# Attention and a gated feed-forward layer on one core: other places for block 2's outputs, GpSimd splits in two runs, a burst one step later, whole weight stores

## The chip, the core and the metric

The kernel runs on one core of a Trainium2 chip. The metric is the device time of one execution in microseconds (us). Before the change three runs took 887.02, 887.28 and 889.04, median 887.28. The engines are TensorE (PE; its weight loads are listed as PEld), VectorE (DVE), ScalarE (ACT), GpSimd (POOL) and SyncE (SP), which issues nearly all transfers. Each engine works through its own instructions in order; semaphores tie the engines together.

## The reference

Attention within chunks of 64 positions (8 batches, 8 heads, 576 positions, head size 64), then a gated feed-forward layer on the 4608 tokens, all in float32.

```python
scores = scale * np.matmul(q_c, k_c.transpose(0, 1, 2, 4, 3))
scores = scores - np.max(scores, axis=-1, keepdims=True)
attn = np.exp(scores)
attn = attn / (np.sum(attn, axis=-1, keepdims=True) + 1e-09)
out = np.matmul(attn, v_c)                                    # -> x, 4608 x 512
...
g = x @ w_gate                                                # 512 -> 1536
silu = g * (1.0 / (1.0 + np.exp(-g)))
val = x @ w_val
return (silu * val @ w_out).astype(np.float32)                # 1536 -> 512
```

## The kernel before

**Blocks and pairs.** The tokens are taken in nine blocks of 512. Blocks 0 and 1 are done in an opening, block 2 alone, and blocks 3 to 8 in three pairs (`b` = 3, 5, 7). While one pair is in its gated layer, the attention of the next pair (`n` in the code, its two halves `c = n.a[0]` and `n.a[1]`) is done beside it; the last pair has none beside it.

**Splits.** Float32 products are made of three TensorE products of rounded parts: a number is split into an upper part (a rounding copy on ScalarE) and a lower one (a subtraction on VectorE or GpSimd). `split`, `Left.lower`, `lower`, `x_lower`, `halves` and `split_sums` are such places.

**Gated steps.** `gated_steps` (L1302) takes a pair through twelve steps `f` = 0 to 11, one for each 128 columns of the hidden layer. A step makes seven products instead of eight (Strassen's scheme on the pair's two blocks), here called product 0 to 6 in TensorE's order: `seventh(ps1, ..., 0)`, `(ps2, ..., 1)`, `(ps1, ..., 2)`, `(ps3, ..., 3)`, `(ps1, ..., 4)`, `(ps2, ..., 5)`, `(ps1, ..., 6)`, each six matmuls of 128x512 (L859). Product 2 goes on in the bank of product 0, and so waits until ScalarE has copied that (`rows`, L1315); likewise product 4 waits for the copy of `v1` (L1319), product 5 for that of `v2` (L1317), and product 6 until VectorE has added product 4 to `v2` (L1328, `add`, L863). VectorE's three adds (L863), two multiplications (`times`, L518) and one split (`hl`, L1193) are each step's own work; ScalarE has three copies, two `Silu`, and the split's copy (`hh`, L1190). `v1` and `v2` lie in one tile whose place is `ts` in even steps and `wo1` in odd ones (L1312).

**The projection lags.** Each step's hidden rows are multiplied by the output weights in the step after (`turns`, `project`, L531; `Left.project`, L1207), in four tiles of 128 tokens. For a pair they add up in the banks `ps_o`. In step 0 of the first pair the projection is that of block 2's last step: it finishes block 2, ScalarE copies each of the four results to `o_sb` (L550) and SP stores it (L551). The copies' buffers came by turns from two pools, `hp` (tag `o_sb`, two buffers, which the weights `left` of odd steps also use) and `ld` (tag `v_t`).

**Bursts.** Next to a step's own work stands the attention of the next pair, by the dictionaries `bursts`, `middle`, `mid` and `behind` of the loop at L1539. A burst is 128 small TensorE products: scores in two of the steps (L291), weighted values in two others (L369). In a step with a burst, the projection's tile 0 stands ahead of product 6, tile 1 behind it, then the burst, then tiles 2 and 3; in another step all four tiles stand ahead of product 6. After a burst of scores ScalarE copies one half of them out of the banks (`take`, L299) and VectorE subtracts the maxima of both (`less_top`, L306, L307). One step later ScalarE does the exponents (`middle`, L312) and VectorE the sums and the division (`normalize`), and in the steps after that VectorE turns the result, eight turns of four transposes each (L356): `mid` is ahead of `hl`, `behind` at the step's end. To some steps belongs a combination of hidden rows on VectorE (`s3`, `s1_of`, L1346), needed after the twelve steps.

**GpSimd.** In block 2 GpSimd prepares combinations of the gate weights (`LateQuarters`). There and beside the first pair's steps 0 to 7 it also prepares six combinations of the output weights: `out_sums` makes the sums, `split_sums` (L1161) splits them, with ScalarE's copy first and GpSimd's subtraction over 128x1024 after it (L1165), and stores them. In the pair's steps the sums stand in even steps and the splits in odd ones.

**Stores of weights.** `save_w` (L198) puts the split gate weights of each `f` into DRAM, from where `load_factors` and `again` fetch them: 1 MB for the first four `f`, and for the other eight only the three quarters that are read later, in two transfers of 512 and 256 KB.

**x of the first pair.** The pair's seven combinations of x are split in block 2's last steps (`pair.x0` to `pair.x6`, `halves`, L1077). Product `i` of a step reads `x[i]`.

**The order.** On PE, ACT and DVE the program's order is the engine's order. The instructions of SP and POOL are placed by a scheduler, which moves a transfer forward when its buffer comes free early.

Of the kernel before, what the change touches and what calls it, by code (L numbers as in the profile page):

```python
# [8 lines left out]
F32 = mybir.dt.float32  # L9
# [5 lines left out]
ALU = mybir.AluOpType  # L15
AX = mybir.AxisListType

P = 128
# [3 lines left out]
DM = H * D  # L22
# [11 lines left out]
def attn_then_gated_ffn(ctx: ExitStack, tc: tile.TileContext, qk, v, wgv, wo, out):  # L34
# [163 lines left out]
    def save_w(f):  # L198
        kept_w[f] = store.tile([P, 2, 4 * Q], F32, name=f"w{f}")
        for at in (slice(0, 4 * Q),) if f < EARLY else (slice(0, 2 * Q), slice(3 * Q, 4 * Q)):  # L200
            nc.sync.dma_start(out=kept_w[f][:, :, at], in_=w_both[f][:, :, at].bitcast(F32))
# [329 lines left out]
    def project(parts, wo_f, which=range(T)):  # L531
# [6 lines left out]
        for t in which:  # L538
            ts, o = slice(t * P, (t + 1) * P), a.o[t]
            nc.tensor.matmul(o, hl[:, ts], woh, start=f == a.steps[0], stop=False)  # L540
            nc.tensor.matmul(o, hh[:, ts], wol, start=False, stop=False)  # L541
            nc.tensor.matmul(o, hh[:, ts], woh, start=False, stop=f == a.steps[1])  # L542
            if f == a.steps[1]:

                pools = (hp, "o_sb"), (ld, "v_t")
                r = a.b * N + t * P

                pool, tag = pools[t % 2]
                o_sb = pool.tile([P, DM], F32, name="o_sb", tag=tag)
                nc.scalar.activation(o_sb, o, AF.Copy, scale=2.0 ** -8)  # L550
                nc.sync.dma_start(out=out[r:r + P, :], in_=o_sb)  # L551
# [609 lines left out]
    def split_sums(j, engine=nc.gpsimd):  # L1161
# [3 lines left out]
        engine.tensor_tensor(out=lo, in0=sums, in1=t, op=ALU.subtract)  # L1165
# [136 lines left out]
    def gated_steps(pair, middle, mid, behind, bursts, nothing=lambda: None):  # L1302
        for f in range(NF):
# [42 lines left out]
            for at, what, j in ((3, pair.s3, 0), (4, pair.s1_of, 0), (8, pair.s3, 1), (9, pair.s1_of, 1), (10, pair.s3, 2)):  # L1346
                if f == at:
                    what(j)
# [143 lines left out]
    def load_late(a):  # L1492
        with tc.issue_after(a.asked):
# [11 lines left out]
              11: lambda: (load_weights(1), load_queries_of(5), pair.x5(), pair.x6())}  # L1505
# [33 lines left out]
    for b in range(3, NB, 2):  # L1539
        n, middle, mid, behind, bursts = None, {}, {}, {}, {}  # L1540
        if b + 2 < NB:
# [6 lines left out]
            bursts = {0: lambda: scores(c, tiles=(q0, q2), first=2), 5: lambda: scores(n.second(), first=2),  # L1548
                      8: lambda: cross(c, first=2), 10: lambda: cross(n.a[1], first=2)}
            middle = {1: lambda: c.exponents(0, NP), 6: lambda: n.a[1].exponents(0, NP)}  # L1550
            mid = {2: turned(c, 0, 1), 3: turned(c, 3, 1), 4: turned(c, 6, 1),
                   7: lambda: turn_some(n.a[1], 0, 1), 8: lambda: turn_some(n.a[1], 3, 1), 9: lambda: turn_some(n.a[1], 6, 1)}
            behind = {1: lambda: c.normalize(0, NP), 2: turned(c, 1, 2), 3: turned(c, 4, 2), 4: turned(c, 7, 1),
                      6: lambda: (n.a[1].normalize(0, NP), load_values(c)), 7: lambda: turn_some(n.a[1], 1, 2),
                      8: lambda: (turn_some(n.a[1], 4, 2), load_values(n.a[1])), 9: lambda: turn_some(n.a[1], 7, 1)}
        if b == 3:
            for i in range(8):
# [37 lines left out]
```

## Time and profile before

| | us |
|---|---|
| runs (three): lowest, median, highest | 887.02, 887.28, 889.04 |
| the profiled execution | 885.88 |
| its span, first to last instruction | 884.1 |
| TensorE busy in the span | 868.6 |
| VectorE, ScalarE, GpSimd busy | 642.0, 418.4, 94.8 |
| first pair's steps 0 to 11 | about 328 to 476 |
| second pair's steps 0 to 11 | about 520 to 661 |

Rows of the timeline read: start in us, duration in us, engine, source line, operation, output<-input, shapes, how often, and in brackets the idle time of the engine ahead of it with what ended it. A row can stand for several like instructions in a run; its start is that of the first one, its duration that of all. In the list of waits the columns are: who waited, for whom, the sum in us, how often, the longest. `SPq` rows are the issues of transfers, not the transfers. In names from the profile the banks of a burst are called `ps_a` wherever they lie.

### The profile page before, as it was taken

What the parts mean: (1) busy time and instruction counts of PE and PEld (TensorE: products, weight loads), DVE (VectorE), ACT (ScalarE), POOL (GpSimd) and SP (SyncE); (2) the same over time, 40 slices, a digit from 0 to 9 for tenths busy, and PEclk for the clock granted to TensorE, in tenths of its full rate; (3) what the DMA queues carried; (4) which work ended last, traced back from release to release, by engine and by line L of the source; (5) the groups of instructions that cost most, each with busy time, mean ns of one, the idle gap of its engine ahead of it and who ended that gap; (6) DMA issues with size and microseconds to landing.
All of it is one profiled execution on the core that took longest, in us unless ns stands there. A gap on an engine that the chain in (4) does not pass through costs nothing.

```text
span 884.1 us, 16286 instructions
## 1 busy us (share of the span) xinstructions
PE 868.6 (98%) x6679; PEld 749.9 (85%) x6679; DVE 642.0 (73%) x898; ACT 418.4 (47%) x609; POOL 94.8 (11%) x72
## 2 busy tenths in 40 slices
PE   7999999999999998999999999999999999999998
PEld 6788888888878787888789998888889988888898
DVE  6888999673888764897977957878769744434674
ACT  5757777543533444435335635334346433333351
POOL 1100000000057722344100000000000000000000
PEclk9999999999999999999999999999999999999999
DMA  9768778888997896788766897565657675555552
GB/s 359 274 249 294 267 282 296 308 285 340 316 356 224 282 327 190 238 268 285 235 202 216 276 298 208 191 212 193 182 207 236 195 225 192 182 200 189 189 187 93
DMA packets 111530, 215.50 MB, mean 244 GB/s; under 512 B 32224, under 2 KB 71648, under 8 KB 102496
## 3 DMA queue, kind: packets, MB, share of 16 engines
q1 hardware_dynamic: 110016, 211.84, 70.5%
q10 hardware_dynamic: 1440, 2.62, 0.8%
q8 instruction: 52, 0.85, 0.4%
q14 instruction: 22, 0.18, 0.1%
HBM read 166.72 MB, written 47.71 MB: 243 GB/s over the span
## 4 chain that ended last, share of the span: by engine, by line
PE 87%; DVE 5%; DMA 4%; ACT 1%; issue 1%; SPq 0%; POOL 0%; DVEq 0%; ACTq 0%
PE ps_a L859 26%; PE ps_gv L859 19%; PE ps_o L1207 14%; PE ps_gv L479 9%; PE ps_gv L1207 6%; PE ps_o L540 3%; PE ps_o L541 3%; PE ps_o L542 3%; DMA qk_t<-in_qk 2%; DVE turned L356 2%; PE ps_a L291 1%; PE ps_a L369 1%; DMA out<-o_sb 1%; DMA t<-th 1%; DVE rows L518 1%
## 5 line engine op out<-in xcount | busy, mean ns | idle before, releaser
L859 PE MATMUL ps_a<-x,factors 128*128 128x512 f32 x864 | 217.2, 391 | 5.1 <-ACT rows L1315 3.0
L859 PEld LDWEIGHTS ps_a<-x,factors 128*128 128x128 f32 x864 | 159.3, 188 | 37.6 <-ACT rows L1315 3.9
L859 PE MATMUL ps_gv<-x,factors 128*128 128x512 f32 x648 | 164.4, 389 | 0.0
L859 PEld LDWEIGHTS ps_gv<-x,factors 128*128 128x128 f32 x648 | 121.6, 188 | 25.3
L479 PE MATMUL ps_gv<-xh,w 128*128 128x512 f32 x320 | 97.9, 391 | 0.2 <-ACT xh L614 0.2
L356 DVE STREAM_TRANSPOSE turned<-s_sb 32x256 f32<-32x256 f32 x192 | 83.6, 436 | 2.6
L1207 PE MATMUL ps_o<-sums,halves 128*128 128x256 f32 x630 | 76.6, 283 | 0.0
L1207 PEld LDWEIGHTS ps_o<-sums,halves 128*128 128x128 f32 x630 | 76.0, 192 | 0.0
L479 PEld LDWEIGHTS ps_gv<-xh,w 128*128 128x128 f32 x320 | 59.8, 188 | 12.9 <-ACT xh L614 0.5
L863 DVE TENSOR_TENSOR rows<-rows,ps_gv 128x512 f32<-128x512 f32 x36 | 24.7, 686 | 59.2 <-PE ps_gv L859 57.6
L518 DVE SCALAR_TENSOR_TENSOR rows<-v,rows 128x512 f32<-128x512 f32 x72 | 55.3, 769 | 12.2 <-ACT rows L1339 5.0
L479 PE MATMUL ps_gv<-xl,w 128*128 128x512 f32 x160 | 61.4, 393 | 0.0
L1190 ACT CAST hh<-rows 128x512 fp32r<-128x512 f32 x36 | 22.3, 620 | 82.3 <-DVE rows L518 82.3
L1250 DVE TENSOR_TENSOR halves<-rows,halves 128x1024 fp32r<-128x1024 f32 x36 | 43.5, 1221 | 18.5 <-ACT halves L1246 18.5
L540 PE MATMUL ps_o<-both,hl 128*128 128x512 f32 x144 | 56.5, 392 | 0.0
L542 PE MATMUL ps_o<-both,hh 128*128 128x512 f32 x144 | 56.1, 389 | 0.0
L541 PE MATMUL ps_o<-both,hh 128*128 128x512 f32 x144 | 56.0, 389 | 0.0
L1207 PE MATMUL ps_o<-left,hh 128*128 128x256 f32 x288 | 53.8, 283 | 0.0
L1207 PE MATMUL ps_gv<-sums,halves 128*128 128x256 f32 x432 | 53.3, 283 | 0.0
L1326 ACT ACTIVATE rows<-rows 128x512 f32<-128x512 f32 x36 | 22.8, 632 | 63.7 <-DVE rows L863 63.6
L1207 PEld LDWEIGHTS ps_gv<-sums,halves 128*128 128x128 f32 x432 | 52.7, 192 | 0.2
L1246 ACT CAST halves<-rows 128x1024 fp32r<-128x1024 f32 x36 | 37.3, 1049 | 28.3 <-PE ps_gv L1207 9.4
(166 smaller groups left out, 1407.4 us busy)
## 6 DMA issues: line engine op xcount, KB each, us to landing
factors<-t SPq DMA_DIRECT2D x36, 1024.0 KB, 7.2
factors<-w SPq DMA_DIRECT2D x36, 512.0 KB, 4.1
sums<-s SPq DMA_DIRECT2D x15, 1024.0 KB, 5.0
t<-th SPq DMA_DIRECT2D x24, 512.0 KB, 4.2
raw<-in_wgv SPq DMA_DIRECT2D x11, 1024.0 KB, 8.7
both<-o SPq DMA_DIRECT2D x22, 512.0 KB, 7.2
qk_t<-in_qk SPq DMA_DIRECT2D x20, 512.0 KB, 7.1
left<-o SPq DMA_DIRECT2D x36, 256.0 KB, 4.5
```

The costliest lines, as they stand in the source:

```text
L356: nc.vector.transpose(out=self.turned[to:to + 32, p:p + 2, j, :, 32 * (i % 2):32 * (i % 2) + 32], in_=src[32 * i:32 * i + 32, :, o // 2, 3 ...
L479: nc.tensor.matmul(ps, w, x, start=first and (k, i) == which[0], stop=last and (k, i) == which[-1])
L518: nc.vector.scalar_tensor_tensor(out=h, in0=pv, scalar=2.0 ** -8, in1=h, op0=ALU.mult, op1=ALU.mult)
L540: nc.tensor.matmul(o, hl[:, ts], woh, start=f == a.steps[0], stop=False)
L541: nc.tensor.matmul(o, hh[:, ts], wol, start=False, stop=False)
L542: nc.tensor.matmul(o, hh[:, ts], woh, start=False, stop=f == a.steps[1])
L859: nc.tensor.matmul(ps, w[u][:, k], x[i][v][:, k], start=first and k == 0 and n == 0, stop=k == NK // 2 - 1 and n == 2, skip_group_check=True)
L863: nc.vector.tensor_tensor(out=t, in0=t, in1=ps, op=ALU.add)
L1207: nc.tensor.matmul(to, a[:, ts], w[:, i], start=first and n == 0, stop=last and n == 2, skip_group_check=True)
L1246: nc.scalar.copy(out=t[:, 0], in_=src)
L1250: nc.vector.tensor_tensor(out=lo, in0=src, in1=hi.bitcast(F32), op=ALU.subtract)
L1326: nc.scalar.activation(h, h, AF.Silu, scale=2.0 ** -8)
```

## The change

Five edits.

1. Block 2's four outputs: tiles 0 and 1 go to the two halves of one tile at `wo1`, tiles 2 and 3 to the two buffers of `v_t`. `hp`'s `o_sb` is left to the weights `left`.
2. `split_sums`: the subtraction on GpSimd is made in two instructions of 128x512 in place of one of 128x1024. All six splits are concerned.
3. The burst of scores for the next pair's first block goes from step 0 to step 1, its exponents from step 1 to 2, its division from 1 to 2, and its eight turns from steps 2 to 4 to steps 3 to 6 (three, three, one, one). The second block's burst stays in step 5, its exponents and division in step 6, its turns in steps 7 to 9. `s1_of(0)` goes from step 4 to step 9. This holds for the first two pairs; the third has no next pair, but its `s1_of(0)` moves too.
4. `save_w` stores every `f` whole, 1 MB in one transfer.
5. The split of the first pair's x[6] goes from block 2's last step into step 0, behind the copy of `v1`.

```diff
     def save_w(f):
         kept_w[f] = store.tile([P, 2, 4 * Q], F32, name=f"w{f}")
-        for at in (slice(0, 4 * Q),) if f < EARLY else (slice(0, 2 * Q), slice(3 * Q, 4 * Q)):
-            nc.sync.dma_start(out=kept_w[f][:, :, at], in_=w_both[f][:, :, at].bitcast(F32))
+        nc.sync.dma_start(out=kept_w[f], in_=w_both[f].bitcast(F32))
...
-                pool, tag = pools[t % 2]
-                o_sb = pool.tile([P, DM], F32, name="o_sb", tag=tag)
+                if a.b != 2:
+                    pool, tag = pools[t % 2]
+                    o_sb = pool.tile([P, DM], F32, name="o_sb", tag=tag)
+                else:
+                    if not t:
+                        a.out = const.tile([P, 2, DM], F32, name="o_sb", tag="wo1")
+                    o_sb = a.out[:, t] if t < 2 else ld.tile([P, DM], F32, name="o_sb", tag="v_t")
                 nc.scalar.activation(o_sb, o, AF.Copy, scale=2.0 ** -8)
                 nc.sync.dma_start(out=out[r:r + P, :], in_=o_sb)
...
-        engine.tensor_tensor(out=lo, in0=sums, in1=t, op=ALU.subtract)
+        for at in (slice(0, 2), slice(2, 4)):
+            engine.tensor_tensor(out=lo[:, at], in0=sums[:, at], in1=t[:, at], op=ALU.subtract)
...
-            for at, what, j in ((3, pair.s3, 0), (4, pair.s1_of, 0), (8, pair.s3, 1), (9, pair.s1_of, 1), (10, pair.s3, 2)):
+            for at, what, j in ((3, pair.s3, 0), (9, pair.s1_of, 0), (8, pair.s3, 1), (9, pair.s1_of, 1), (10, pair.s3, 2)):
...
-              11: lambda: (load_weights(1), load_queries_of(5), pair.x5(), pair.x6())}
+              11: lambda: (load_weights(1), load_queries_of(5), pair.x5())}
...
-            bursts = {0: lambda: scores(c, tiles=(q0, q2), first=2), 5: lambda: scores(n.second(), first=2),
+            bursts = {1: lambda: scores(c, tiles=(q0, q2), first=2), 5: lambda: scores(n.second(), first=2),
                       8: lambda: cross(c, first=2), 10: lambda: cross(n.a[1], first=2)}
-            middle = {1: lambda: c.exponents(0, NP), 6: lambda: n.a[1].exponents(0, NP)}
-            mid = {2: turned(c, 0, 1), 3: turned(c, 3, 1), 4: turned(c, 6, 1),
+            middle = {2: lambda: c.exponents(0, NP), 6: lambda: n.a[1].exponents(0, NP)}
+            mid = {3: turned(c, 0, 1), 4: turned(c, 3, 1), 5: turned(c, 6, 1), 6: turned(c, 7, 1),
...
-            behind = {1: lambda: c.normalize(0, NP), 2: turned(c, 1, 2), 3: turned(c, 4, 2), 4: turned(c, 7, 1),
+            behind = {2: lambda: c.normalize(0, NP), 3: turned(c, 1, 2), 4: turned(c, 4, 2),
...
         if b == 3:
+            middle[0] = pair.x6
             for i in range(8):
                 behind[i] = sums_behind(i, behind.get(i, lambda: None))
```

The engines' orders at the places that the prediction speaks of. ScalarE in the first pair's step 0, before; `rows<-ps_a` in the list is `Silu` of product 6, `s_sb<-ps_a` the copy of the burst's scores, and the last row is step 1's first copy:

```order
L62 CAST x<-s_sb 128x1024 x2
L1315 COPY rows<-ps_a 128x512
L1317 COPY v<-ps_gv 128x512
L1319 COPY v<-ps_a 128x512
L1326 ACTIVATE rows<-rows 128x512
L1190 CAST hh<-rows 128x512
L550 ACTIVATE o_sb<-ps_o 128x512
L1339 ACTIVATE rows<-ps_a 128x512
L550 ACTIVATE o_sb<-ps_o 128x512
L299 COPY s_sb<-ps_a 128x8x64 x2
L550 ACTIVATE o_sb<-ps_o 128x512 x2
L1315 COPY rows<-ps_a 128x512
```

The same place now:

```order
L62 CAST x<-s_sb 128x1024
L1320 COPY rows<-ps_a 128x512
L1322 COPY v<-ps_gv 128x512
L1324 COPY v<-ps_a 128x512
L62 CAST x<-s_sb 128x1024
L1331 ACTIVATE rows<-rows 128x512
L1195 CAST hh<-rows 128x512
L554 ACTIVATE o_sb<-ps_o 128x512 x4
L1344 ACTIVATE rows<-ps_a 128x512
L1320 COPY rows<-ps_a 128x512
```

One split of x has moved behind the three copies, the four outputs stand together, and the copy of the scores has left the step. VectorE at the change from step 4 to step 5 (of both pairs), before; the adds to `rows` and `v` (L863) begin a step's work, L1224 is a combination of hidden rows, here `s1_of(0)`, and `top` is the burst's first maximum:

```order
L1193 TENSOR_TENSOR hl<-rows,hh 128x512
L518 SCALAR_TENSOR_TENSOR rows<-v,rows 128x512
L356 STREAM_TRANSPOSE turned<-s_sb 32x2x4x32 x4
L1224 TENSOR_TENSOR rows<-rows 128x1024
L863 TENSOR_TENSOR rows<-rows,ps_gv 128x512
L863 TENSOR_TENSOR v<-v,ps_a 128x512
L863 TENSOR_TENSOR v<-v,ps_gv 128x512
L518 SCALAR_TENSOR_TENSOR rows<-v,rows 128x512
L1193 TENSOR_TENSOR hl<-rows,hh 128x512
L518 SCALAR_TENSOR_TENSOR rows<-v,rows 128x512
L306 TENSOR_REDUCE top<-ps_a 128x8
```

And now:

```order
L1198 TENSOR_TENSOR hl<-rows,hh 128x512
L517 SCALAR_TENSOR_TENSOR rows<-v,rows 128x512
L355 STREAM_TRANSPOSE turned<-s_sb 32x2x4x32 x8
L867 TENSOR_TENSOR rows<-rows,ps_gv 128x512
L867 TENSOR_TENSOR v<-v,ps_a 128x512
L867 TENSOR_TENSOR v<-v,ps_gv 128x512
L517 SCALAR_TENSOR_TENSOR rows<-v,rows 128x512
L355 STREAM_TRANSPOSE turned<-s_sb 32x2x4x32 x4
L1198 TENSOR_TENSOR hl<-rows,hh 128x512
L517 SCALAR_TENSOR_TENSOR rows<-v,rows 128x512
L305 TENSOR_REDUCE top<-ps_a 128x8
```

Step 4 ends with two turns in place of one turn and the combination `s1_of(0)`, and step 5 has a turn between the multiplication and `hl`, ahead of the burst's maxima. Last, SP around block 2's outputs, before; `factors` are the weights of step 2, `v_t` values for the next pair's attention:

```order
L1130 DMA factors<-w_818 128x2x512
L1130 DMA factors<-w_818 128x2x256
L1130 DMA factors<-t_3147 128x2048
L551 DMA out<-o_sb 128x512 x2
L271 DMA v_t<-in_v 128x4x64
L551 DMA out<-o_sb 128x512 x2
```

And now:

```order
L1134 DMA factors<-w_818 128x2x512
L1134 DMA factors<-w_818 128x2x256
L555 DMA out<-o_sb 128x512 x3
L1134 DMA factors<-t_3139 128x2048
L555 DMA out<-o_sb 128x512
L270 DMA v_t<-in_v 128x4x64
```

Three of the four stores now go ahead of the last part of the weights (1 MB). Further ahead on SP, in block 2, one transfer of `left` (256 KB, step 3's) now stands before the loads of the first pair's second block, as its buffer no longer serves for an output.

## The prediction

> **What bounds the kernel now.** The page first: TensorE is busy for nearly the whole span, so the end moves only by what TensorE waits, or by work that comes to wait in front of it.
>
> ```profile
> span 884.1 us, 16286 instructions
> PE 868.6 (98%) x6679; PEld 749.9 (85%) x6679; DVE 642.0 (73%) x898; ACT 418.4 (47%) x609; POOL 94.8 (11%) x72
> ```
>
> The list of waits with TensorE as the one that waits (columns: sum in us, times, longest) then says what those waits are. These are its rows outside the opening:
>
> ```profile
> PE ps_a L859 <- ACT rows L1315: 3.0, 2, 2.7
> PE ps_a L291 <- DMA qk_t<-in_qk: 1.5, 3, 0.6
> PE ps_a L859 <- DVE v L863: 1.4, 1, 1.4
> ...
> PE ps_a L369 <- DVE h L518: 1.0, 1, 1.0
> ...
> PE ps_a L859 <- ACT s_sb L299: 0.7, 1, 0.7
> ...
> PE ps_a L291 <- ACT rows L1339: 0.2, 1, 0.2
> ```
>
> Of the 1.5 only one wait (0.6) lies outside the opening. So some 6.9 us in all can be won (3.0 + 0.6 + 1.4 + 1.0 + 0.7 + 0.2). The timeline shows where each comes from. First the first pair's steps 0 and 1:
>
> ```profile
> 329.88 1.05 ACT L62 CAST x<-s_sb 128x1024 fp32r<-128x1024 f32 x1 [1.76 <-DMA t<-th]
> ...
> 339.27 0.34 SPq L1130 DMA_DIRECT2D factors<-t  x1
> ...
> 339.97 1.31 SPq L551 DMA_DIRECT2D out<-o_sb  x2
> ...
> 347.34 1.08 ACT L550 ACTIVATE o_sb<-ps_o 128x512 f32<-128x512 f32 x2 [4.22 <-DMA out<-o_sb]
> ...
> 348.95 1.66 PE L859 MATMUL ps_a<-x,factors 128*128 128x512 f32 x6 [2.71 <-ACT rows L1315]
> ```
>
> Block 2's third output needs the buffer of its first, whose store is on the way, so ScalarE stands still for 4.22 with the copies of step 1 behind it, and TensorE loses 2.71. The other 0.3 of that row is step 0: the split of x[6] (the first line) waits for a store, and the copy `rows` stands behind it. Then steps 7 and 8 of that pair:
>
> ```profile
> 423.39 0.68 DVE L863 TENSOR_TENSOR v<-v,ps_a 128x512 f32<-128x512 f32 x1
> ...
> 424.13 3.01 PE L859 MATMUL ps_a<-x,factors 128*128 128x512 f32 x12
> ...
> 425.38 1.78 DVE L356 STREAM_TRANSPOSE turned<-s_sb 32x256 f32<-32x256 f32 x4
> ...
> 427.63 2.51 POOL L1165 TENSOR_TENSOR sums<-sums 128x1024 fp32r<-128x1024 f32 x1 [9.28 <-ACT sums L1164]
> 427.80 2.89 DVE L518 SCALAR_TENSOR_TENSOR rows<-v,rows 128x512 f32<-128x512 f32 x1
> ...
> 435.65 1.65 PE L859 MATMUL ps_a<-x,factors 128*128 128x512 f32 x6 [1.36 <-DVE v L863]
> ```
>
> Product 6 of a step rewrites the bank that VectorE's add of v2 reads. In step 7 that add ends at 424.07 and the product starts at 424.13: no room at all, and no loss. In step 8 VectorE comes 1.36 late, after standing 2.2 beside GpSimd's split (2.89 for an operation of 0.69). Last, the second pair's burst in step 0, which has no projection behind it to cover ScalarE's copy of the scores:
>
> ```profile
> 533.42 1.66 PE L859 MATMUL ps_a<-x,factors 128*128 128x512 f32 x6 [0.73 <-ACT s_sb L299]
> ```
>
> **What the change takes away.** The outputs' new places end the 4.22, if the stores land in time (rival A): -2.71. x[6] behind the step's third copy: -0.3; its 1.05 on ScalarE and an operation on VectorE then lie beside products 3 to 5, and it is first read by product 6. The burst in step 1 has two tiles of projection behind it, as the burst of step 5 has, and that one costs nothing; in the second pair this saves 0.73 and the 0.2 of the list's last row, 0.93. The rows of step 5's burst in the first pair, in which no wait stands before TensorE's two products, and the burst itself (in the second pair):
>
> ```profile
> 402.82 0.69 DVE L307 TENSOR_TENSOR s_sb<-ps_a,top 128x512 f32<-128x512 f32 x1
> ...
> 403.48 1.60 PE L859 MATMUL ps_a<-x,factors 128*128 128x512 f32 x6
> ...
> 404.92 1.53 PE L859 MATMUL ps_gv<-x,factors 128*128 128x512 f32 x6
> ```
> ```profile
> 587.82 2.10 PE L291 MATMUL ps_a<-qk_t 64*64 64x64 f32 x128
> ```
>
> For the split in runs of 512, what matters is whether VectorE gets in between two GpSimd instructions. It does so in step 6:
>
> ```profile
> 413.05 1.29 POOL L1156 TENSOR_TENSOR sums<-right 128x512 f32<-128x512 f32 x1
> ...
> 413.63 1.26 DVE L518 SCALAR_TENSOR_TENSOR rows<-v,rows 128x512 f32<-128x512 f32 x1 [0.95 <-ACT rows L1326]
> ...
> 414.42 1.62 POOL L1157 TENSOR_TENSOR sums<-sums 128x512 f32<-128x512 f32 x1
> ...
> 415.58 1.02 DVE L1193 TENSOR_TENSOR hl<-rows,hh 128x512 fp32r<-128x512 f32 x1 [0.69 <-ACT hh L1190]
> ```
>
> VectorE started at 413.63, waited for the GpSimd operation to end (414.34) and was done 0.55 later, while GpSimd's next one took 1.62 against 1.29. So a collision costs VectorE at most a run of about 1.3 instead of one of 2.5: some 1.2 less, which is nearly all of step 8's 1.36. [...]
>
> The same helps in block 2, where x's halves wait for a split:
>
> ```profile
> 296.47 3.39 POOL L1165 TENSOR_TENSOR sums<-sums 128x1024 fp32r<-128x1024 f32 x1
> ...
> 300.87 0.68 DVE L518 SCALAR_TENSOR_TENSOR h<-ps_gv,h 128x512 f32<-128x512 f32 x1
> ...
> 301.60 2.08 PE L369 MATMUL ps_a<-turned,v_t 64*64 64x64 f32 x124 [0.99 <-DVE h L518]
> ```
>
> But VectorE's operation reads the product that TensorE makes right before this multiplication, which it reached at 301.60 - 0.99 = 300.61, so the operation's 0.68 stays: I count 0.3 of the 0.99 (none to 0.99). Removed: 2.71 + 0.3 + 1.36 + 0.3 + 0.93 = 5.6.
>
> **What it adds.** Each thing that moved a step later now stands nearer to something else on VectorE. Two rows price it: the combination s3 that now stands with three turns right after the normalizing, and the projection's four tiles that TensorE does ahead of product 6 in a step without a burst (one tile of them, 0.36, in a step with one).
>
> ```profile
> 384.90 1.23 DVE L1224 TENSOR_TENSOR rows<-rows 128x1024 f32<-128x1024 f32 x1
> ```
> ```profile
> 448.85 1.43 PE ps_o L1207 x12
> ```
>
> First pair. Steps 1 to 4 now repeat what steps 5 to 8 were: burst, normalizing, three turns, three turns. Step 3 is like step 7: no loss. Step 4 is like step 8, with 1.23 more for s3, 1.2 less for the runs, and product 6 coming 1.07 later: 1.36 + 1.23 - 1.2 - 1.07 = 0.3. Its lateness is not made up before step 5, whose product 6 comes after one tile again: I put 0.6 (0 to 1.0). Step 5 has a new turn (1.78) ahead of the scores' maxima; 0.69 of it fills a wait for `hh`, so 1.1 shows. The bank that TensorE wants next was free at 402.82 + 0.69 = 403.51 and is taken at 404.92: 1.4 of room, no loss. Step 6's new turn again adds 1.1, of which it covers some 0.3 of the waits for GpSimd, and step 7 had no room: 0.8 (0.2 to 1.3). Step 8 keeps 1.36 - 1.2 = 0.2 (0 to 0.5). Sum 1.9, bounds 0.2 to 3.6.
>
> Second pair: no GpSimd, and room in step 7. The add of v2 ends at 609.81 and TensorE takes the bank at 611.31, 1.5 later, more than 1.1: nothing. `s1_of(0)` in step 9 is another 1.23, but that step has two turns where steps 3, 4 and 8 have three, 1.78 less: nothing.
>
> ```profile
> 609.13 0.68 DVE L863 TENSOR_TENSOR v<-v,ps_a 128x512 f32<-128x512 f32 x1
> ...
> 611.31 2.91 PE L859 MATMUL ps_a<-x,factors 128*128 128x512 f32 x12
> ```
>
> Whole weight stores: eight stores carry 256 KB more, eight issues fall away. TensorE waits for no transfer until the scores in block 2 (the 0.6). Ahead of that load go one store and, by the new order on SP, one `left` of 256 KB. Rows of the page, the issues and the timeline:
>
> ```profile
> GB/s 359 274 249 294 267 282 296 308 285 340 316 356 224 282 327 190 238 268 285 235 202 216 276 298 208 191 212 193 182 207 236 195 225 192 182 200 189 189 187 93
> ```
> ```profile
> w<-w SPq DMA_DIRECT2D x8, 256.0 KB, 6.1
> ```
> ```profile
> 243.48 1.22 SPq L201 DMA_DIRECT2D w<-w  x2
> ```
>
> At the 356 GB/s of that slice 256 KB are 0.74, twice 1.5; one issue less gives back about 0.6 to 0.8. I take +0.7 (-0.2 to 1.5). [...]
>
> **Sum.** -5.6 + 1.9 + 0.7 = -3.0. The profiled execution took 885.88 (span 884.1, 1.78 around it), so it would come to 882.9; it lies 1.4 under the median of the runs, 887.28, and the same 3.0 from the median gives **884.3**.
>
> **Rivals.**
> A. The wait is only moved. The outputs of tiles 0 and 1 now lie in the buffer that step 1's v1 and v2 use. If their stores land as late as they did, ScalarE stands in step 1 before v2. Landing of the first two outputs, and of the last two, as the transfers' rows have it:
>
> ```profile
> DMA to landing us min/median/max: 6.9/7.1/7.3
> ```
> ```profile
> DMA to landing us min/median/max: 2.4/2.6/2.8
> ```
>
> TensorE reached product 2 of step 1 at 348.95 - 2.71 = 346.24; two products later (1.44 each, 403.48 to 404.92), without the burst's 2.10 and step 0's 0.3, it wants v1 at 346.7, and two copies of 0.54 (347.34) come ahead: the second store, issued near 341, may land at 345.6 without loss. After 7.1 it lands at 348.1 and TensorE loses 2.5 again: 886.8. For it: the 7.1. Against: those stood behind 1 MB of `factors` (issued 339.27), which the new order puts behind three of the outputs. Chance 0.12.
> B. GpSimd keeps what VectorE waits for through both runs. Steps 4 and 8 then lose 1.2 each more and block 2's 0.3 stays: 884.3 + 2.7 = 887.0. Against: 413.63 to 414.42. Chance 0.12.
> C. VectorE becomes the bound (slower). If steps 4 to 8 have no idle time to take s3 and the two turns, all of 1.23 + 1.78 + 1.78 = 4.79 shows, in both pairs 9.58: 887.28 - 5.6 + 0.7 + 9.58 = 892.0. It ends slower by over 0.3% once more than 7.6 of the 9.58 shows (2.7 + 5.6 - 0.7). For: no room in step 7. Against: 1.5 of room in the second pair, and the 0.69 before `hl`. Chance 0.07.
> D. VectorE takes it all: the new waits are near 0.2 and the transfers nothing. 887.28 - 5.6 + 0.2 = 881.9. For: VectorE idles 0.69 in each step. Chance 0.15.
>
> **Numbers.** My forecast keeps 0.54. A measurement can tell 0.3%, 2.7 us; the forecast's own bounds (-5.6 + 0.2 - 0.2 = -5.6 to -5.6 + 3.6 + 1.5 = -0.5) straddle that, and I put two thirds of it beyond. Faster: 0.36 + 0.15 = 0.51; same: 0.18 + 0.12 + 0.12 = 0.42; slower 0.07. Range 881.8 to 887.5: from D up to A and B with half a microsecond of spread, leaving out C.
>
> **What would show it.** In the changed kernel's list of waits: no `o_sb` waiting for `out`; TensorE's wait for `rows` L1315 gone, or, with A, one for v's copy in step 1 near 347; no wait for `s_sb` near 533; VectorE operations beside a split at about 1.9 instead of 2.9 (with B still 2.9); TensorE's waits for v L863 in steps 4, 5 and 7 of the first pair together 1 to 2.5. If those sum to over 5, C is right; if VectorE never holds TensorE up, D.

## The result and the profile after

The changed kernel takes 881.26 us in the median of six runs (880.29 to 883.23); the kernel before, run beside it, takes 887.15 (884.29 to 889.04, six runs). The ratio is 0.9937, 95% interval 0.9918 to 0.9956: 5.9 us faster, where 3.0 was forecast. On the two other chips where both were run again, the changed kernel took 881.25 and 881.09 us and the kernel before 889.63 and 888.87; the ratios there are 0.9910 (0.9892 to 0.9927) and 0.9916 (0.9893 to 0.9939). Four runs of the experiments lay far out of line (1002 and 2227 us of the kernel before, 4756 of outputs_only, 2320 of quarters_in_512) and are left out of every median and ratio here.

The profiled execution of the changed kernel took 883.23, the longest of its six runs. From the page of the changed kernel, the span and the engines' busy time:

```profile
span 881.4 us, 16285 instructions
...
PE 868.7 (99%) x6679; PEld 750.5 (85%) x6679; DVE 639.6 (73%) x898; ACT 418.7 (48%) x609; POOL 99.2 (11%) x78
```

The spans differ by 2.7 (884.1 before), the medians by 5.9. So the two profiles hold less than half of the gain between them, and the rest has to be looked for in executions that they don't show. First what they show: the changed kernel's list of waits with TensorE waiting (columns as before: sum in us, times, longest).

```profile
PE ps_a L290 <- DMA qk_t<-in_qk: 3.9, 3, 1.6
...
PE ps_a L863 <- DVE v L867: 1.1, 2, 0.8
...
PE ps_a L368 <- DVE h L517: 0.8, 1, 0.8
```

The 3.0 for `rows`, the 0.7 for `s_sb` and the 0.2 of the second burst have gone. The waits for VectorE's adds to v stand at 1.1 in all, where 1.4 stood before. The waits for the queries have grown from 1.5 to 3.9; more on that below. The timeline of the changed kernel in the first pair's step 0 and at the start of step 1:

```profile
334.86 1.05 ACT L62 CAST x<-s_sb 128x1024 fp32r<-128x1024 f32 x1
...
340.77 2.06 ACT L554 ACTIVATE o_sb<-ps_o 128x512 f32<-128x512 f32 x4
...
341.39 1.34 SPq L555 DMA_DIRECT2D out<-o_sb  x3
...
342.82 0.41 SPq L1134 DMA_DIRECT2D factors<-t  x1
...
345.30 0.59 ACT L1322 COPY v<-ps_gv 128x512 f32<-128x512 f32 x1 [0.81 <-PE ps_gv L863]
```

The first row is the split of x[6], now in step 0. The four outputs are copied in one go. Three stores are issued before the 1 MB of `factors`, where both of the first two stood behind it before. The copy of v2, which overwrites the first outputs' place, waits for its own product and for no store. The landing of those three stores:

```profile
DMA to landing us min/median/max: 2.2/2.4/2.7
```

2.2 to 2.7 us, where the first two took 6.9 to 7.3. The fourth store, which still stands behind `factors`, took 6.4. GpSimd's split in step 8, now in two runs, and VectorE's multiplication beside it, from the same timeline:

```profile
427.28 3.10 POOL L1170 TENSOR_TENSOR sums<-sums 128x512 fp32r<-128x512 f32 x2 [11.62 <-ACT sums L1168]
427.45 1.78 DVE L517 SCALAR_TENSOR_TENSOR rows<-v,rows 128x512 f32<-128x512 f32 x1
```

VectorE's multiplication is done at 429.23, before GpSimd's second run ends (430.38): 1.78 in place of 2.89. The two waits for VectorE that are left in the first pair, in steps 4 and 8:

```profile
388.13 3.01 PE L863 MATMUL ps_a<-x,factors 128*128 128x512 f32 x12 [0.82 <-DVE v L867]
...
434.19 1.66 PE L863 MATMUL ps_a<-x,factors 128*128 128x512 f32 x6 [0.26 <-DVE v L867]
```

TensorE's idle time in both profiles, stretch by stretch, gives the spans' difference: step 1 -2.71, step 0 -0.31, the second pair's burst -0.98 (0.73 + 0.24), the first pair's steps -0.28 (1.36 to 1.08), block 2's wait for `h` -0.18 (0.99 to 0.81), together -4.46; and in the other direction the queries in block 2, 0.55 to 1.38, and the opening, 5.42 to 6.21 in the first 40 us, together +1.62. That makes -2.84, beside -2.7 by the spans.

### The profile page after: what moved, and what is told of

The parts are those of the page before. It is cut to its first block, busy times and chain, and to the rows that moved or that the text cites. A ratio compares the mean times of both kernels' runs of the same rounds, so it can differ in the third digit from the quotient of the medians.

```text
span 881.4 us, 16285 instructions
## 1 busy us (share of the span) xinstructions
PE 868.7 (99%) x6679; PEld 750.5 (85%) x6679; DVE 639.6 (73%) x898; ACT 418.7 (48%) x609; POOL 99.2 (11%) x78
## 4 chain that ended last, share of the span: by engine, by line
PE 89%; DVE 6%; DMA 3%; issue 1%; ACT 1%; SPq 0%; DVEq 0%; ACTq 0%
PE ps_a L863 26%; PE ps_gv L863 19%; PE ps_o L1212 14%; PE ps_gv L478 10%; PE ps_gv L1212 6%; PE ps_o L539 3%; PE ps_o L540 3%; PE ps_o L541 3%; DVE turned L355 3%; PE ps_a L290 2%; PE ps_a L368 1%; DMA raw<-in_wgv 1%; DMA qk_t<-in_qk 1%; DVE rows L517 1%; PE ps_a L468 0%
## 5 line engine op out<-in xcount | busy, mean ns | idle before, releaser
L863 PE MATMUL ps_a<-x,factors 128*128 128x512 f32 x864 | 217.2, 391 | 1.2 <-DVE v L867 1.1
L863 PEld LDWEIGHTS ps_a<-x,factors 128*128 128x128 f32 x864 | 159.3, 188 | 33.1 <-DVE v L867 1.8
L863 PE MATMUL ps_gv<-x,factors 128*128 128x512 f32 x648 | 164.4, 389 | 0.0
L863 PEld LDWEIGHTS ps_gv<-x,factors 128*128 128x128 f32 x648 | 121.6, 188 | 25.4
```

Of the source, the lines that this page charges most:

```text
L863: nc.tensor.matmul(ps, w[u][:, k], x[i][v][:, k], start=first and k == 0 and n == 0, stop=k == NK // 2 - 1 and n == 2, skip_group_check=True)
```

## The experiments

Three theories stood at the start. **S**: the gain is the sum of the waits removed, one by one, and my sizes for what is added were too large. **W**: the whole weight stores pay for something. **N**: the profiles lack something in the opening. A fourth came up with the clock of the single runs, **G**, and with the first traces a fifth, **Q**; they are named where they arise. Every ratio is to runs of the kernel before on the same chip.

**outputs_only.** The kernel before with edit 1 alone.

```
-                pool, tag = pools[t % 2]
-                o_sb = pool.tile([P, DM], F32, name="o_sb", tag=tag)
+                if a.b != 2:
...
+                    o_sb = a.out[:, t] if t < 2 else ld.tile([P, DM], F32, name="o_sb", tag="v_t")
```

> The kernel before with nothing but the new places of block 2's outputs. Theory S (the change gains what the removed waits cost, one by one): ScalarE's wait of 4.2 us for the first output's store and TensorE's 2.71 us behind it are gone, the other waits stay; time 2.4 to 3.0 us below the kernel before, about 884.4 us. Rival M (the wait only moves, to step 1's v1 and v2): a new wait near 345 us, gain under 1 us, about 886.5 us. Rival L (the transfers of the outputs, spread less in time, also take something off later loads): gain over 3.5 us.

886.00 us against 889.29 (eleven and nineteen runs): ratio 0.9974 (0.9957 to 0.9991), 2.3 us by the ratio. The time is near S, the mechanism is M's. The timeline of this kernel:

```profile
339.75 0.34 SPq L1135 DMA_DIRECT2D factors<-t  x1
340.44 4.81 SPq L556 DMA_DIRECT2D out<-o_sb  x4
...
349.69 0.58 ACT L1322 COPY v<-ps_gv 128x512 f32<-128x512 f32 x1 [3.69 <-DMA out<-o_sb]
...
350.81 0.50 PE L864 MATMUL ps_a<-x,factors 128*128 128x512 f32 x1 [1.36 <-ACT v L1324]
```

The stores still stand behind the load of `factors`, and ScalarE waits 3.69 for them at the next user of the place, the copy of v2: rival A of the prediction, at half its price (1.36). It starts two products later than the wait it replaces; that this is what is gained is argued, not shown.

**burst_in_first.** The changed kernel with the bursts' tables and `s1_of(0)` as before.

```
-            bursts = {1: lambda: scores(c, tiles=(q0, q2), first=2), ...
+            bursts = {0: lambda: scores(c, tiles=(q0, q2), first=2), ...
(middle, mid, behind and s1_of(0) as in the kernel before)
```

> The changed kernel with the first burst of each pair, what follows from it and the combination s1 in their old steps. My forecast: the second pair's 0.93 us of waiting comes back, and 1.9 us of new VectorE waits in the first pair go: 1.0 us below the changed kernel, about 880.3 us. Theory S, by the waits of the changed kernel's trace (0.82 in step 4 gone, 0.26 in step 8 perhaps): 0.93 - 0.82 to 0.93 - 1.08, no difference that can be seen, 881.3 us. Rival P (moving the burst is worth more than its waits): over 1 us above the changed kernel.

882.46 us, ratio 0.9933 (0.9914 to 0.9953); its profiled execution took 885.21. All three expectations had the outputs' places do their work without the burst's move. They don't. The timeline:

```profile
337.09 0.34 SPq L1134 DMA_DIRECT2D factors<-t  x1
337.72 4.67 SPq L555 DMA_DIRECT2D out<-o_sb  x4
...
348.92 0.59 ACT L1322 COPY v<-ps_gv 128x512 f32<-128x512 f32 x1 [5.58 <-DMA out<-o_sb]
...
350.04 2.08 PE L863 MATMUL ps_a<-x,factors 128*128 128x512 f32 x6 [3.25 <-ACT v L1324]
```

With the burst in step 0 the stores stand behind `factors` again, land after 8.0 to 10.5 us, and TensorE waits 3.25: in this execution, rival A in full. It was the longest of the six runs and the only one with a mean clock under 1.0; the median lies 1.2 above the changed kernel's 881.25 on another chip, so the other five, which have no profile, most likely lost less. The six matmuls behind the wait take 2.08 where six such matmuls take 1.66 behind other waits. The windows of this execution show why (columns: window, length, TensorE busy and its matmuls, granted clock, share and GB/s of the transfers):

```profile
348.00:350.00 2.00, 0.00 (x0) 1.00 0.05 20
350.00:352.00 2.00, 1.96 (x7) 0.77 0.42 96
352.00:354.00 2.00, 2.00 (x6) 0.50 0.55 125
354.00:356.00 2.00, 2.00 (x15) 0.88 0.19 41
```

The granted clock falls to 0.50 behind the wait. That gave two theories. **Q**: what lets the stores land early is their place on SP's queue, which the burst's move sets, not the buffers. **G**: a long wait of TensorE costs more than its length, since the clock falls after it.

**stores_in_two and split_in_one** ran with these two. The first is the changed kernel with edit 4 undone:

```
-        nc.sync.dma_start(out=kept_w[f], in_=w_both[f].bitcast(F32))
+        for at in (slice(0, 4 * Q),) if f < EARLY else (slice(0, 2 * Q), slice(3 * Q, 4 * Q)):
+            nc.sync.dma_start(out=kept_w[f][:, :, at], in_=w_both[f][:, :, at].bitcast(F32))
```

> The changed kernel with each weight store in two parts again (three quarters of the bytes, two issues). If the whole stores cost the 0.7 us that I forecast for them: 0.7 us below the changed kernel, about 880.6 us, with TensorE's wait for the queries in block 2 shorter by as much. Theory S with whole stores free: equal to the changed kernel within 0.5 us, 881.3 us. Rival W (the whole stores are where the gain over the forecast came from): 1.0 to 1.5 us above the changed kernel, about 882.6 us.

880.93 us, ratio 0.9913 (0.9896 to 0.9931). W is unlikely; 0.7 and nothing can't be told apart, since the changed kernel wasn't run on that chip. It was repeated beside it (below).

The second is the changed kernel with edit 2 undone:

```
-        for at in (slice(0, 2), slice(2, 4)):
-            engine.tensor_tensor(out=lo[:, at], in0=sums[:, at], in1=t[:, at], op=ALU.subtract)
+        engine.tensor_tensor(out=lo, in0=sums, in1=t, op=ALU.subtract)
```

> The changed kernel with GpSimd's split as one instruction of 128x1024 again. Theory S: VectorE's operations beside a split take 2.9 us again where they took 1.1 to 1.8; TensorE's wait for v in step 8 of the first pair grows from 0.26 to about 1.4 us, the one in step 4 from 0.82 to 1.5 to 2.0 us, the one for h in block 2 from 0.81 to about 1.0 us: 2.0 to 2.5 us above the changed kernel, about 883.5 us. Rival B (the two runs hold VectorE as long as one): no difference, 881.3 us.

883.14 us, ratio 0.9937 (0.9916 to 0.9958), 1.9 above the changed kernel's 881.25 on another chip; the two ratios' intervals overlap, so the waits have to decide. TensorE's waits in its timeline:

```profile
301.84 2.11 PE L368 MATMUL ps_a<-turned,v_t 64*64 64x64 f32 x124 [1.33 <-DVE h L517]
...
386.89 3.02 PE L863 MATMUL ps_a<-x,factors 128*128 128x512 f32 x12 [1.18 <-DVE v L867]
...
434.09 1.67 PE L863 MATMUL ps_a<-x,factors 128*128 128x512 f32 x6 [1.36 <-DVE v L867]
```

Step 8 is back at its 1.36 exactly, step 4 and block 2 each lose more. Theory S; rival B is out.

**before_again, after_again.** No edit: both kernels profiled once more, the second also timed.

> The kernel before, unchanged, profiled once more. Theory G (the long wait of step 1 costs more than its 2.71 us, because TensorE's granted clock falls after it in most runs): if this execution has a mean clock under 1.0, the clock is at half for some 3 to 4 us right behind the wait of step 1, and the execution takes 887 us or more; if the clock is 1.0, it takes about 886 us, as the first profile did. Rival N (what the first profile lacks lies in the transfers of the opening): clock 1.0 throughout and longer waits for the queries.

This execution took 888.79 us with a mean clock of 0.998. The timeline of step 1:

```profile
348.38 1.08 ACT L550 ACTIVATE o_sb<-ps_o 128x512 f32<-128x512 f32 x2 [5.52 <-DMA out<-o_sb]
...
350.00 1.93 PE L859 MATMUL ps_a<-x,factors 128*128 128x512 f32 x6 [4.01 <-ACT rows L1315]
```

And its windows behind that wait, columns as above:

```profile
351.00:352.00 1.00, 1.00 (x4) 0.62 0.97 342
352.00:353.00 1.00, 1.00 (x3) 0.50 0.59 133
353.00:354.00 1.00, 1.00 (x4) 0.50 0.84 243
354.00:355.00 1.00, 1.00 (x5) 0.67 0.83 200
355.00:356.00 1.00, 1.00 (x6) 1.00 0.41 90
```

The same wait is 4.01 here where the first profile had 2.71 (the stores took 8.2 to 8.6 us to land, not 6.9 to 7.3), and 0.38 + 0.50 + 0.50 + 0.33 = 1.71 us of clock are lost behind it. Step 1 cost this execution 5.7 us, twice what my sum removed: from product 1 of step 1 to product 1 of step 2 TensorE took 16.92 us (344.46 to 361.38), 2.94 more than in the first profile (13.98), and the whole execution took 2.91 more. The first profile had a mean clock of 1.0. It was the exception: of the 80 runs of the kernel before that the experiments' comparisons use, two had 1.0 (886.95 and 885.97 us) and all others 0.998 or less. Theory G holds in this execution, whose waits for the queries come to 0.5 in all, so N is out; that the fall stands behind step 1 in the other runs too is likely, but only this one has a profile.

> The changed kernel, unchanged, profiled and timed once more, as the base for the others. Theory G: mean clock 1.0 in all runs, median 881 to 882 us, TensorE's waits for v in the first pair 0.2 to 1.1 us in all, the waits for transfers in the opening and block 2 between 1.5 and 3.9 us. Rival N: the first profile's 3.9 us for the queries are typical of the changed kernel, and the clock is below 1.0 as often as in the kernel before.

881.25 us (880.38 to 882.45), ratio 0.9910 (0.9892 to 0.9927), clock 0.999 to 1.0 in all six runs. Its list of waits:

```profile
PE ps_a L290 <- DMA qk_t<-in_qk: 1.9, 3, 0.9
PE ps_a L863 <- DVE v L867: 1.5, 3, 1.0
...
PE ps_a L368 <- DVE h L517: 0.4, 1, 0.4
```

The 3.9 for the queries was one execution's; here it is 1.9, all of it in the opening. As the instructions of the opening are the same in both kernels, I take its spread (TensorE idle 4.6 to 6.3 us in the first 40 over all profiles) for chance in the transfers.

**one_long_gap, two_short_gaps, three_small_gaps, eight_tiny_gaps.** G by itself: the changed kernel with ScalarE's copy of product 0 repeated, in steps of the last pair, where nothing else waits. The repeats write the same values.

```
-            nc.scalar.copy(out=h, in_=ps1)
+            for _ in range(1 if bursts else {4: 11}.get(f, 1)):
+                nc.scalar.copy(out=h, in_=ps1)
(the others: {4: 7, 8: 7}, {4: 5, 6: 5, 8: 5} and {f: 4 for f in range(2, 10)})
```

> The changed kernel with ScalarE's copy of product 0 made 11 times over in step 4 of the last pair, which has nothing else to wait for: TensorE gets one gap of about 4.1 us (10 more copies at 0.48, less 0.7 of room). Theory G (a gap this long brings the clock down for some 3.4 us, which costs half of that): 4.1 + 1.7 = 5.8 us above the changed kernel, mean clock 0.998. Rival N (a gap costs its length and no more): 4.1 us above, clock 1.0.

> The changed kernel with that copy made 7 times over in steps 4 and 8 of the last pair: two gaps of about 2.2 us (6 more copies at 0.48, less 0.7), 4.4 us in all, slightly more than the one long gap. Theory G: 4.4 us above the changed kernel, clock 1.0, and so about 1.4 us faster than the one long gap. Rival N: 0.3 us slower than the one long gap.

> The changed kernel with the repeated copy 5 times over in steps 4, 6 and 8 of the last pair: at 0.616 us for each further copy, three gaps of about 1.8 us, 5.4 us in all, beside the one gap of 5.49 us measured before. Theory G (only a gap near 3 us or longer can bring the clock down): clock 1.0 at all three, 5.0 to 5.5 us above the changed kernel, about 886.5 us, 1 us or more under the one long gap although the gaps add up to the same. Rival N (a gap costs its length and no more): the same as the one long gap, 887.8 us.

A repeated copy took 0.616 us and not 0.48, so the first two kernels' gaps came out longer than planned. One gap of 5.49: 887.79 us, 6.5 above the changed kernel (881.25), clock 0.996 or less in all ten runs. Two gaps of 3.02: 890.35, 9.1 above, clock 0.994 to 0.998. Three gaps of 1.79: 886.13, 4.9 above, clock 1.0 or 0.999 in three of five runs, 0.997 and 0.998 in two. The long gap, from the first kernel's timeline, and both gaps of the second, from its own:

```profile
750.12 2.93 PE L863 MATMUL ps_a<-x,factors 128*128 128x512 f32 x6 [5.49 <-ACT rows L1321]
```

```profile
748.95 1.66 PE L863 MATMUL ps_a<-x,factors 128*128 128x512 f32 x6 [3.02 <-ACT rows L1321]
...
796.18 2.93 PE L863 MATMUL ps_a<-x,factors 128*128 128x512 f32 x6 [3.02 <-ACT rows L1321]
```

Two gaps of one length in one execution: six matmuls take 1.66 behind the first and 2.93 behind the second. And the third kernel, windows around its first gap:

```profile
745.50:746.00 0.50, 0.00 (x0) 1.00 0.89 377
...
747.00:747.50 0.50, 0.50 (x3) 0.89 0.04 16
747.50:748.00 0.50, 0.50 (x2) 0.50 0.00 0
...
750.50:751.00 0.50, 0.50 (x3) 0.70 0.00 0
```

A gap of 1.79 (up to 746.04) brought the clock to a half from 747.4 to 750.8; the other two gaps of that execution did not. So rival N of these kernels (a gap costs its length and no more) is out, and my limit "near 3 us" too: a gap of 1.8 can do it, one of 3.0 need not. The stretches at half, read from the windows, are 3.4 us long (this one, 351.2 to 354.7 in before_again, 351.1 to 354.5 in burst_in_first) or 6.8 (747.7 to 754.5 in the long gap's kernel and 795.3 to 802.1 with the second 3.02). The three of 3.4 begin 1.0 to 1.4 us behind their gap's end, the two of 6.8 inside the gap. Why a stretch is 3.4 or 6.8 is open, and so is why one of two gaps of 3.02 brings the clock down and the other does not. The last kernel has eight gaps, each shorter than any that a fall came with:

> The changed kernel with the repeated copy 4 times over in steps 2 to 9 of the last pair: at 0.616 us for each further copy, eight gaps of about 1.18 us, 9.4 us of idle time in all, more than any other kernel here. [...] Rival T (each gap has a chance to bring the clock down that grows with its length, and three gaps of 1.79 did so in two runs of five): the clock under 0.999 in half of the runs or more, and 891.5 us or more. Rival I (it is the idle time as such): clock 0.995 or less, 893 us or more.

892.74 us, ratio 1.0032 (1.0018 to 1.0046), and the clock at 1.0 or 0.999 in all twelve runs, against T and I. In the time, the changed kernel's 881.25 and the 9.4 us of the listed gaps make 890.65, too low by 2 us, as a gap costs more than the wait that is listed (T's 891.5 us or more would fit the time, but not the clock). The same product in two steps that follow each other:

```profile
725.58 1.65 PE L863 MATMUL ps_a<-x,factors 128*128 128x512 f32 x6 [1.18 <-ACT rows L1321]
738.03 1.65 PE L863 MATMUL ps_a<-x,factors 128*128 128x512 f32 x6 [1.17 <-ACT rows L1321]
```

A step takes 12.45 with a gap and 10.98 without (from the copy of product 0 to the next step's, in the changed kernel): 1.47 for a listed 1.18. In the same way the gaps of 1.79 and 3.02 behind which the clock stayed up lengthen their steps by 2.09 and 3.31. Over the same nine steps of the last pair, and so free of what differs elsewhere, the four kernels are longer than the changed kernel (98.82) by 7.86, 9.37, 7.90 and 11.75 us; less 0.3 for each gap, that leaves 2.1, 2.7 and 1.6 us for the one fall in each of the first three, and nothing in the last.

**outputs_back.** The changed kernel with edit 1 undone (outputs_only's diff the other way).

> The changed kernel with block 2's outputs in their old places; the burst stays in step 1. Theory Q (it is the order on SP's queue, which the burst's move changed, that makes the first stores land in about 2.5 us instead of 7 to 9): the third output waits for the first store, but only until about 344 us, some 2 us instead of 4.2 or more; TensorE loses 0 to 1.5 us in step 1, the clock stays at 1.0: 881.5 to 882.8 us. Rival E (each edit is worth its own wait, as my sum had it): the 2.71 us are back, with the clock's fall behind them in most runs: 884 us at clock 1.0, 886 us with the fall.

882.20 us (881.31 to 883.20), ratio 0.9918 (0.9905 to 0.9931): 1.0 above the changed kernel's 881.25 (same chip, not side by side). Clock 0.999 or 1.0. Theory Q, not E (each edit worth its own wait, 884 or more). The timeline:

```profile
340.96 1.09 ACT L549 ACTIVATE o_sb<-ps_o 128x512 f32<-128x512 f32 x2 [2.02 <-DMA out<-o_sb]
...
343.07 1.66 PE L858 MATMUL ps_a<-x,factors 128*128 128x512 f32 x6 [0.65 <-ACT rows L1315]
```

The old places cost 2.02 of ScalarE's time and 0.65 of TensorE's, once the stores go ahead of `factors`.

**outputs_and_burst.** The kernel before with edits 1 and 3 alone.

> The kernel before with the outputs' new places and the first burst in step 1, and nothing else (no split in runs, no whole stores, x[6] in its old step). Theory Q with G: no wait in step 1, clock 1.0, the first stores land in 2 to 3 us; the split's waits stay (about 1.4 us in step 8, some in step 4, 1.0 to 1.5 us in block 2) and the 0.3 us of x[6]: 1.5 to 3 us above the changed kernel, 883 to 884 us. Rival W (the whole stores and the runs carry the gain over the forecast): 885 us or more.

884.51 us, ratio 0.9936 (0.9921 to 0.9951), 3.3 above the changed kernel, a little over the range given. What is left in its timeline:

```profile
331.86 1.67 PE L864 MATMUL ps_a<-x,factors 128*128 128x512 f32 x6 [0.88 <-ACT rows L1320]
...
388.32 3.02 PE L864 MATMUL ps_a<-x,factors 128*128 128x512 f32 x12 [1.79 <-DVE v L868]
...
435.69 1.66 PE L864 MATMUL ps_a<-x,factors 128*128 128x512 f32 x6 [1.36 <-DVE v L868]
```

In this execution the split in one piece costs more than it did before the burst moved, since step 4 loses 1.79 as well, as it lost 1.18 in split_in_one. The profile of burst_only, the next kernel, has the same split and the same burst and no such wait in step 4, so that the runs of 512 pay for the burst's move is likely but not shown.

**burst_only.** The kernel before with edit 3 alone.

> The kernel before with the first burst of each pair in step 1 (and s1 in step 9), the outputs in their old places. Theory Q (the burst's move puts the outputs' stores ahead of the load of the factors): the third output waits about 2 us instead of 4 to 5.5, TensorE loses 0.5 to 1 us there, the clock does not fall; 0.5 to 1 us above the two edits together (884.5 us), so about 885.3 us, 4 to 5 us below the kernel before, more than the outputs' places alone gave (3.2 us). Rival E (each edit its own wait): only the second pair's 0.93 us go and new waits of 1 to 2 us come, no faster than the kernel before, with the wait of 2.7 to 4 us still in step 1.

885.39 us against 888.87: ratio 0.9957 (0.9940 to 0.9974), 3.8 us by the ratio, a little under the 4 to 5 expected. The timeline:

```profile
340.49 0.84 SPq L551 DMA_DIRECT2D out<-o_sb  x2
341.83 0.33 SPq L1130 DMA_DIRECT2D factors<-t  x1
...
343.04 1.09 ACT L550 ACTIVATE o_sb<-ps_o 128x512 f32<-128x512 f32 x2 [2.09 <-DMA out<-o_sb]
...
345.15 1.66 PE L859 MATMUL ps_a<-x,factors 128*128 128x512 f32 x6 [0.63 <-ACT rows L1315]
```

The burst's move alone takes the wait of 2.7 to 4.0 us down to 0.63. By the traces the two edits are two ways at one wait: the places alone leave 1.36 of it, the burst alone 0.63, both together nothing. The times fit this less sharply: 2.3 us for the places alone, 3.8 for the burst alone and some 5.7 for both by the ratios, which nearly add up, since the burst's move also ends the second pair's waits and brings new ones; undone from the changed kernel, each costs only 1.0 to 1.2.

**after_third, stores_in_two_again, x6_back.** On one chip: the changed kernel; the same with stores_in_two's diff; the same with edit 5 undone:

```
-              11: lambda: (load_weights(1), load_queries_of(5), pair.x5())}
+              11: lambda: (load_weights(1), load_queries_of(5), pair.x5(), pair.x6())}
...
-            middle[0] = pair.x6
```

> The changed kernel once more, as the base for the two that follow: 881 to 881.5 us, clock 1.0.

> The changed kernel with each weight store in two parts, on one chip with the changed kernel. If whole stores cost the 0.7 us of my sum: 0.7 us below the changed kernel. If they cost nothing: within 0.4 us of it. Rival W: 1 us or more above it.

> The changed kernel with x[6] split in block 2's last step again. My sum: 0.3 us above the changed kernel, TensorE waiting for ScalarE's first copy in step 0 of the first pair. By the 0.88 us that this wait had in the kernel with the outputs and the burst alone: 0.9 us above. Rival X (the split of x[6] now stands in nobody's way): no difference.

881.09, 881.04 and 881.75 us; ratios 0.9916 (0.9893 to 0.9939), 0.9912 (0.9896 to 0.9928) and 0.9911 (0.9895 to 0.9927). The whole stores cost nothing that can be seen, though the intervals would hide 0.7. One run of the changed kernel took 885.64 at a clock of 0.998: of its 18 runs on the three chips, the only one under 0.999. x[6] stays open in the time: the medians differ by 0.7, the ratios not at all. In the traces TensorE's wait in step 0 varies where x[6] is split in block 2's last step: 0.31 and nothing in the two profiles of before, 0.53 in outputs_only, 0.74 in burst_only, 0.88 in outputs_and_burst, nothing in x6_back. With the split in step 0 no profile has it.

**quarters_in_512.** The changed kernel with the late quarters' 128x1024 operations on GpSimd in runs of 512 too.

```
-            self.engine.tensor_tensor(out=self.t, in0=w[:, 0], in1=w[:, 1], op=ALU.add)
+            for k in range(0, 4 * Q, N):
+                self.engine.tensor_tensor(out=self.t[:, k:k + N], in0=w[:, 0, k:k + N], in1=w[:, 1, k:k + N], op=ALU.add)
(and the split in lower() likewise)
```

> The changed kernel with the remaining 128x1024 operations of GpSimd in block 2 (the late quarters' sum and split) in runs of 512 too. Theory S: only block 2's wait for h (0.4 to 0.8 us in the changed kernel) can still fall, by 0.2 to 0.5 us: 880.8 to 881.3 us. Rival D2 (VectorE's other waits in block 2 reach the end too): over 1 us below the changed kernel.

880.77 us (three runs), ratio 0.9896 (0.9881 to 0.9910); the wait for `h` is 0.34, where the changed kernel's three profiles have 0.81, 0.42 and 0.53. The time can't be told from the changed kernel's 881.25. It is the kernel I would keep, but no gain is shown.

## Why the prediction was wrong

The direction was right, and nearly every wait that I said would go went. The value was 3.0 us too high, and the range ended half a microsecond too high at its low end. Two errors of about the same size, both in what was added or taken as the base.

**The base.** The step that failed: "it lies 1.4 under the median of the runs, 887.28, and the same 3.0 from the median gives 884.3". I took the 1.4 for a spread that both kernels share. It was part of what the change removes: the profiled execution had a short wait (2.71) and no fall of the clock behind it; before_again shows 4.01 and 1.71 more, and the clock of 0.998 or less in 78 of 80 runs says that the median has such falls in it (the clocks of the six runs beside the changed kernel are not on record). Worked from the profiled execution itself, with the sizes measured since, the sum comes out: 2.71 + 0.31 + 1.36 + 0.40 + 0.98 = 5.76 removed and 1.22 added give 885.88 - 4.54 = 881.34, where 881.26 was measured. That it comes within a tenth is luck: with the 0.3 us that a wait costs beyond its listed length, some 0.7 more would go (four waits less, one or two more).

**Removed, term by term.** The wait in step 1, -2.71: right in size for the profiled execution, too small for before_again, and put down to the outputs' places alone. "The outputs' new places end the 4.22, if the stores land in time" leaves out that it is the burst's move that puts the stores ahead of `factors` and so makes them land in time (outputs_only has them behind it, burst_only ahead); the row for it (the stores ahead of `factors`) was in the prediction, but only as an argument against rival A. Step 8, -1.36 with 0.2 left: 0.26, 0.25 and 0.26 in the three profiles. The second pair's burst, -0.93: 0.98. Block 2, -0.3: from 0.99 to 0.59 in the mean (0.81, 0.42, 0.53), and too small, as the six profiles with the split in one piece have 0.99 to 2.03. x[6], -0.3: between nothing and 0.88 in the traces, open in the time.

**Added.** VectorE in the first pair, +1.9: TensorE's waits for v come to 1.08, 1.53 and 1.06 in the three profiles, 1.22 in the mean. The step that was mis-sized is the carrying over: I let step 4's lateness reach step 5 whole (0.6) and step 7 keep 0.8, and found 0.08 and 0.52 in the mean, for 0.37 in step 4 (0.3 forecast). Whole stores, +0.7: nothing seen (881.04 beside 881.09). The wait for the queries in block 2 is between 0 and 1.4 with whole stores and between 0 and 0.9 with stores in two, from one execution to the next, so my 0.6 from one profile was no measure of the load on that queue.

**The rivals.** A was given 0.12 and does not occur in the changed kernel, but it is real: undo the burst's move and it is there (3.25 in the one execution profiled). B is refuted by split_in_one. C is refuted by the list of waits. D names about the right time, 881.9, and half of its reason: the transfers cost nothing, VectorE still holds TensorE up by 1.2.

## What to carry to other kernels

The wait for a store's landing had two handles here, the buffer (new places alone left 1.36 of TensorE's 2.7 to 4.0 us) and the store's place in the issuing queue (the burst's move alone left 0.63). Look at what stands ahead of it there: the stores ahead of the 1 MB of `factors` landed after 2.2 to 2.8 us in the profiles of the changed kernel and of burst_only, and those issued within 5 us behind it after 6.1 to 10.5 in those of before, before_again, outputs_only, burst_in_first and the changed kernel. Where a wait of some 1.8 us or more stands before TensorE (the shortest that a fall came with here was 1.79), look at the granted clock in the microseconds behind it, and if the profiled execution is faster than the median, ask whether the median pays something that this profile doesn't show before its terms are taken from the median.

## What the runs showed of the hardware

That the clock falls in a kernel with TensorE busy for 98% was not expected, nor that 1.8 us of waiting can be enough: stretches of 3.4 or 6.8 us at half the granted clock came with gaps of 1.79, 3.02, 3.25, 4.01 and 5.49 us, and none with eight gaps of 1.18, or with the 2.71 in the first profile of before. The length of a gap alone does not decide: in the same executions another gap of 3.02 and two more of 1.79 brought no fall, and what else decides was not shown. By its mean clocks, 0.998 or less in 78 of 80 runs (0.002 of 885 is 1.8), the kernel before lost an estimated 1.8 us or more in nearly every run, if its falls lie where TensorE is busy, as in before_again. A wait of TensorE cost some 0.3 us more than its listed length (2.09 for 1.79). And VectorE's multiplication of 0.69 took 1.78 beside two GpSimd runs of 512 that stand directly behind each other, and was done before the second one ended; beside one of 1024 it took 2.89.
